# Strassen products also in the down projection of the second MoE, for two couples of token blocks

## The chip, the cores and the metric

The kernel runs on one core of a Trainium2 chip. The metric is device time in microseconds (us) of one execution; lower is better. The engines are TensorE (PE, matrix products), VectorE (DVE), ScalarE (ACT), GpSimd (POOL) and SyncE (SP, which here issues every DMA). Each of them works through its own queue of instructions in order.

## The reference

Attention with a decaying bias (batch 4, 8 heads, 576 positions, head width 64) gives 2304 tokens of width 512. Two feed-forward layers follow; the change lies in the second.

```python
def _moe_ref(x, w_gate, w_val, w_out, rms_g):          # first MoE, d_ff 1536
    xn = x / rms * rms_g
    g = xn @ w_gate
    silu = g * (1.0 / (1.0 + np.exp(-g)))
    return silu * (xn @ w_val) @ w_out
...
def _moe2_ref(x, w_in, w_out):                          # second MoE, d_ff 2048
    h = x @ w_in                                        # 512 -> 2048
    g = h - np.tanh(h)
    return g @ w_out                                    # 2048 -> 512
```

## The kernel before

The tokens are cut into 6 blocks of 384 (`NBLK`, `TB`), held transposed: features on the 128 partitions, 384 tokens in the columns. Every operand of a large product is split into two fp16 halves, and `mm3` (L692) makes a product as three matmuls of 128x128 weights by 384 columns: high by high, high by low, low by high. In code order the attention's last tiles and blocks 0 to 5 of the first MoE come first, then the second MoE. A scheduler in the framework reorders instructions within what data and buffers allow when the program is built, and the order it fixes is the order of the queues; `order` in the section on the change is that order.

**First MoE.** `up1_g` and `up1_v` make one 128-row piece of the hidden layer each (12 matmuls); the DVE ends each by one operation on the temporary `tm` (L712, L722), ACT takes the high half `sh` (L723) and POOL the low half `sl` (L724). `down1` makes an output piece from 36 matmuls and stores it to DRAM (`x2d`, L734).

**Weights of the second MoE.** `w_in` and `w_out` come as 64-bit floats, 16 pieces each of 128x512 numbers (512 KB a load, L557). `decode` turns a piece into fp32 by three DVE operations (L559 to L561); an ACT square (L250) sums it up for a scale; `split` writes the fp16 halves (ACT L575, DVE L576) into the slots of two large tiles, `WI` and `W2`. All of this is a list of small tasks (`w2_tasks`) that are run between the 28 product groups of block 5 of the first MoE, the rest in block 0 of the second.

**Second MoE.** Blocks 0 and 1 are ordinary: `up2` (16 pieces of 12 matmuls; ACT tanh, DVE L1256, ACT high half, DVE L1258 low half into `DH`, `DL`) and `down2` (4 output pieces of 48 matmuls, ACT L1271, store L1272). Blocks 2/3 and 4/5 are taken as couples. On the way up `pair_up` uses Strassen's scheme with seven products in place of eight for the 2x2 blocks of weights and tokens: for each of 8 pieces `s8` seven products of 6 matmuls, put together by DVE (L1302), tanh on ACT (L1288), DVE L1289, high half ACT L1290, low half POOL L1291. The sums of weight blocks that it needs (S1 to S4) are made by DVE from the halves (`form_tasks`, L1182 and on) into the tile `SF`, the sums of token blocks by `x2_forms`. On the way down the couples use the ordinary `down2`, 2 blocks x 4 pieces x 48 = 384 matmuls a couple.

Strassen's scheme in this form makes four output blocks from seven products: one product of the sums S1 and T1 goes into two of the outputs, S2 and S3 likewise.

## Time and profile before

| | us |
|---|---|
| median of 3 runs | 1069.54 |
| lowest, highest | 1068.47, 1090.91 |
| span of the profiled execution | 1066.9 |
| median less span | 2.6 |
| PE busy | 971.0 |
| DVE busy | 680.1 |
| ACT busy | 606.2 |
| POOL busy | 325.6 |

The span runs from the first to the last instruction of the profiled execution. Matmuls overlap in the pipeline of the PE, so the mean length of a row (0.33 us) is twice the step from one matmul to the next. An engine's idle time matters only where a later engine had to wait for it.

### The profile page before, as it was taken

Reading aid. Unit: us, or ns where it says so; the run is one execution under the profiler, and the core shown is the slowest. Engines: PE = TensorE matmul, PEld = TensorE weight load, DVE = VectorE, ACT = ScalarE, POOL = GpSimd, SP = SyncE. Lnnn points to the kernel's source line nnn. Section 1 sums busy time; section 2 is a strip of 40 time slices with the busy share of each in tenths; the row PEclk is TensorE's granted clock in tenths of the full one; section 3 lists DMA queues with packets and bytes.
Section 4 is the critical chain, followed back from the end, with each engine's and each line's share of the span. In section 5 each row is a group of like instructions: output and inputs, shape, how many; then the busy total and the mean of one; then the engine's idle time right before and its main releaser. Section 6 shows DMA issues by size and latency. Waiting matters only on the chain.

```text
span 1066.9 us, 19296 instructions
## 1 busy us (share of the span) xinstructions
PE 971.0 (91%) x7471; PEld 616.9 (58%) x7472; DVE 680.1 (64%) x1472; ACT 606.2 (57%) x1172; POOL 325.6 (31%) x405
## 2 busy tenths in 40 slices
PE   1488967798899999999999899999999999999998
PEld 1377645455566666666667555655666666666664
DVE  8986998975585641674553878579792683438500
ACT  6589657776665763776766446446571462225400
POOL 5121275423462541364356112100200251015200
PEclk9986989999999999999999999999999999999999
DMA  8614524241211112210100960131102000000000
GB/s 269 257 36 108 191 72 144 65 132 38 64 27 53 25 44 74 77 28 21 54 19 11 309 233 1 46 135 68 60 1 82 8 2 16 23 23 1 8 23 30
DMA packets 49439, 76.81 MB, mean 72 GB/s; under 512 B 25891, under 2 KB 35203, under 8 KB 48835
## 3 DMA queue, kind: packets, MB, share of 16 engines
q1 hardware_dynamic: 49346, 75.58, 22.7%
q8 instruction: 58, 0.95, 0.4%
q14 instruction: 35, 0.28, 0.1%
HBM read 59.42 MB, written 9.55 MB: 65 GB/s over the span
## 4 chain that ended last, share of the span: by engine, by line
PE 63%; DVE 15%; DMA 9%; ACT 6%; issue 4%; POOL 2%; SPq 1%; ACTq 0%; DVEq 0%; POOLq 0%
PE m L693 11%; PE m L695 11%; PE m L694 11%; PE mm L693 7%; PE mm L695 7%; PE mm L694 7%; DVE w L560 1%; PE pv L494 1%; PE st L452 1%; PE st L453 1%; DMA wo<-wv 1%; DMA raw<-wo 1%; DMA w<-wo 1%; DVE w L559 1%; DMA qst<-qa 1%
## 5 line engine op out<-in xcount | busy, mean ns | idle before, releaser
L693 PE MATMUL mm<-xth,w 128*128 128x384 f16 x480 | 158.0, 329 | 28.2 <-DVE tm L712 20.9
L694 PE MATMUL mm<-xtl,w 128*128 128x384 f16 x480 | 157.9, 329 | 0.6 <-DMA xtl<-xl 0.6
L695 PE MATMUL mm<-xth,w 128*128 128x384 f16 x480 | 157.5, 329 | 0.1
L694 PEld LDWEIGHTS <-w 128*128 128x128 f16 x960 | 94.4, 98 | 87.1 <-issue 32.7
L693 PEld LDWEIGHTS <-w 128*128 128x128 f16 x960 | 94.9, 99 | 62.7 <-ACT w L575 3.7
L695 PEld LDWEIGHTS <-w 128*128 128x128 f16 x960 | 94.2, 98 | 63.5 <-issue 2.5
L693 PE MATMUL m<-dh,w 128*128 128x384 f16 x384 | 124.0, 326 | 0.7 <-ACT t L1271 0.7
L694 PE MATMUL m<-dl,w 128*128 128x384 f16 x384 | 124.4, 326 | 0.0
L695 PE MATMUL m<-dh,w 128*128 128x384 f16 x384 | 124.0, 326 | 0.0
L474 POOL TENSOR_TENSOR phl<-pf,phl 128x512 f16<-128x512 f32 (+2 forms) x90 | 97.8, 1094 | 40.1 <-ACT phl L467 38.7
L724 POOL TENSOR_TENSOR sl<-tm,sh 128x384 f16<-128x384 f32 x72 | 74.8, 1039 | 112.9 <-ACT sh L723 105.6
L462 POOL TENSOR_SCALAR_AFFINE_SELECT pf<-pf 128x128 f32<-128x128 f32 (+3 forms) x105 | 46.9, 449 | 175.0 <-ACT pf L460 174.7
L1263 POOL TENSOR_SCALAR io<-iso,isd 128x1 f32<-128x1 f32 x24 | 12.0, 501 | 258.8 <-ACT t L1271 258.8
L460 ACT ACTIVATE pf<-st,lnp,ilam 128x512 f32<-128x512 f32 (+2 forms) x105 | 73.0, 703 | 23.0 <-PE st L453 17.9
L1271 ACT ACTIVATE t<-m,io 128x384 f32<-128x384 f32 x24 | 13.8, 578 | 126.1 <-PE m L695 123.0
L693 PE MATMUL mm<-sh,wo 128*128 128x384 f16 x240 | 77.9, 326 | 2.3 <-DVE tm L712 2.3
L695 PE MATMUL mm<-sh,wo 128*128 128x384 f16 x240 | 78.1, 326 | 0.5 <-DVE wo L576 0.5
L694 PE MATMUL mm<-sl,wo 128*128 128x384 f16 x240 | 78.1, 326 | 0.0
L452 PE MATMUL st<-q,kl 128*128 128x128 f16 (+1 forms) x456 | 62.9, 217 | 8.6 <-DVE q L368 2.7
L1302 DVE SCALAR_TENSOR_TENSOR c<-m,sigma,c 128x768 f32<-128x768 f32 x32 | 32.5, 1015 | 57.3 <-PE m L695 55.6
L1291 POOL TENSOR_TENSOR dl<-c,dh 128x768 f16<-128x768 f32 x28 | 48.0, 1731 | 54.9 <-ACT dh L1290 54.9
L712 DVE SCALAR_TENSOR_TENSOR tm<-tm,mm 128x384 f32<-128x384 f32 x60 | 32.8, 547 | 43.9 <-ACT tm L711 41.4
(369 smaller groups left out, 2582.1 us busy)
## 6 DMA issues: line engine op xcount, KB each, us to landing
raw<-wo SPq DMA_DIRECT2D x16, 512.0 KB
w<-win SPq DMA_DIRECT2D x16, 512.0 KB
wo<-wg SPq DMA_DIRECT2D x12, 512.0 KB
wo<-wv SPq DMA_DIRECT2D x12, 512.0 KB
stk<-kt SPq DMA_DIRECT2D x4, 1152.0 KB
x2d<-tm SPq DMA_DIRECT2D x24, 192.0 KB
x2f<-x2d SPq DMA_DIRECT2D x6, 768.0 KB
out<-t SPq DMA_DIRECT2D x24, 192.0 KB
```

Source lines behind the costliest of these rows:

```text
L452: P.matmul(out=ps[:, o:o + w], lhsT=K2[sl][:, ks], rhs=q2_of(T)[:, h, 0:w], start=True, stop=False)
L460: A.activation(out=pf[:, 0:o], in_=ps[:, 0:o], func=ACTF.Exp, scale=bstate[b]["ilam"][:, hh:hh + 1], bias=lnp)
L462: G.affine_select(out=dg, in_=dg, pattern=[[0, len(heads)], [1, w]], compare_op=ALU.is_ge, fill=0.0, base=0, channel_multiplier=-1)
L474: G.tensor_tensor(out=u["pl"][:, 0:n], in0=u["pf"][:, 0:n], in1=u["ph"][:, 0:n], op=ALU.subtract)
L693: P.matmul(out=ps, lhsT=wh, rhs=xh, start=first, stop=False)
L694: P.matmul(out=ps, lhsT=wh, rhs=xl, start=False, stop=False)
L695: P.matmul(out=ps, lhsT=wl, rhs=xh, start=False, stop=last)
L712: V.scalar_tensor_tensor(out=t, in0=t, scalar=1.0, in1=ps, op0=ALU.add, op1=ALU.mult)
L724: moe_pend.append(lambda: G.tensor_tensor(out=SH["l"][:, f, :], in0=t, in1=SH["h"][:, f, :], op=ALU.subtract))
L1271: A.activation(out=t, in_=ps, func=ACTF.Copy, scale=io)
L1291: by.tensor_tensor(out=DL[:, s8, ds, :], in0=c[:, ds], in1=DH[:, s8, ds, :], op=ALU.subtract)
L1302: V.scalar_tensor_tensor(out=out, in0=ps, scalar=sg, in1=c0, op0=ALU.mult, op1=ALU.add)
```

## The change

The couples' down projection is made by Strassen's scheme too (`pair_down`): seven products, each for two output pieces `e` and of 24 matmuls, 336 in place of 384 a couple. That needs the sums of `w_out`'s blocks, and sums of the blocks of the gated hidden layer (`g_forms`). All forms of the weights are now made once, from the fp32 pieces rather than from the halves, written to DRAM (`keep_form`: 28 stores of 256 KB into `wi_d`, 28 into `wo_d`) and read back for the couples through three rotating buffers each (`wr`, 917 KB a load, 16 loads; `wd`, 1 MB, 14 loads). 24 fp32 pieces are parked in DRAM (`pk_d`, 256 KB each) and read again when their sums are made (`sum_tasks`). The sums are cut into tasks, and `newest` makes the scheduler place each behind the newest instruction of DVE and ACT. The order becomes up of block 0, up of block 1, down of block 0, down of block 1, then the couples. Products that are added up stay in one PSUM bank (`acc`), others get banks of their own. WI and W2 take memory in which the normalised tiles `xh`, `xl` of the attention lie.

```diff
+    pk_d = [dram.tile([128, 512], FP32, name=f"pk{i}") for i in range(24)]
+    wi_d = [dram.tile([4, 128, 7, 2, 256], FP16, name=f"wid{i}") for i in range(2)]
+    wo_d = [dram.tile([128, 2, 8, 256], FP16, name=f"wod{i}") for i in range(7)]
...
+    def put(to, t, s):
+        t4 = t.rearrange("p (c w) -> p c w", c=4)
+        A.activation(out=to[:, :, 0, :], in_=t4, func=ACTF.Copy, scale=s)
+        V.scalar_tensor_tensor(out=to[:, :, 1, :], in0=t4, scalar=s, in1=to[:, :, 0, :], op0=ALU.mult, op1=ALU.subtract)
+
+    def keep_form(i, g, k, q, t):
+        if i == 0:
+            SY.dma_start(out=wi_d[g][:, :, q, k].rearrange("c p w -> p c w"), in_=t.rearrange("p c h w -> p c (h w)"))
+        else:
+            SY.dma_start(out=wo_d[q][:, g, 4 * k:4 * k + 4], in_=t.rearrange("p c h w -> p c (h w)"))
...
+        def piece(i, g, k):
+            W, n = (WI, W2)[i], slot_of(g, k)
+            if i == 0:
+                raw = raw_slots(W2, 2 * (n % 4))
...
+            decode(slot_f(W, n), (win, wo2)[i][g, :, k], raw)
...
+            if i == 1 or g % 2:
+                SY.dma_start(out=parked(i, g, k), in_=slot_f(W, n))
...
+        def load(i, g, k):
+            for nm, gg, kk in (("a21", g + 2, k), ("a22", g + 2, k + 2), ("a11", g, k), ("a12", g, k + 2)):
+                d[nm] = in_p.tile([128, 512], FP32, name=nm, tag=nm)
+                SY.dma_start(out=d[nm], in_=parked(i, gg, kk))
...
+        def first(i, g, k):
+            d["t"] = in_p.tile([128, 512], FP32, name="sft", tag="sft")
+            G.tensor_tensor(out=d["t"], in0=d["a21"], in1=d["a22"], op=ALU.add)
+            G.tensor_tensor(out=d["a21"], in0=d["a11"], in1=d["a21"], op=ALU.subtract)
...
+        def third(i, g, k):
+            V.tensor_tensor(out=d["t"], in0=d["t"], in1=d["a11"], op=ALU.subtract)
+            form(i, g, k, S2, d["t"])
+            V.tensor_tensor(out=d["a12"], in0=d["a12"], in1=d["t"], op=ALU.subtract)
+            form(i, g, k, S4, d["a12"])
...
+    def newest():
+        st = ExitStack()
+        for e in (V, A):
+            st.enter_context(tc.issue_after(next(i for i in reversed(nc.cur_bb.bb.instructions) if i.engine == e.engine)))
+        return st
...
+    for f in range(16):
+        up2(0, f)
+        run_tasks(w2t, 1)
...
+    for f in range(16):
+        up2(1, f)
+        if f % 2:
+            with newest():
+                run_tasks(sums, 1)
+    for i, d in enumerate(D_ORDER):
+        with newest():
+            run_tasks(sums, 3)
+        down2(0, d)
+        if i == 0:
+            x2_stat(2)
+        if i == 1:
+            x2_forms(2)
...
+    def g_forms(p, s8):
+        c = CR[:, c_at(p, s8)]
+        V.tensor_tensor(out=c[:, 0:2], in0=c[:, 1:4:2], in1=c[:, 0:2], op=ALU.subtract)
+        V.tensor_tensor(out=c[:, 3], in0=c[:, 3], in1=c[:, 0], op=ALU.subtract)
+        V.tensor_tensor(out=c[:, 2], in0=c[:, 2], in1=c[:, 3], op=ALU.subtract)
+        t = g_form(p, s8)
+        A.activation(out=t[:, :, 0, :], in_=c, func=ACTF.Copy)
+        for e, fs in ((V, slice(0, 2)), (G, slice(2, 4))):
+            e.tensor_tensor(out=t[:, fs, 1, :], in0=c[:, fs], in1=t[:, fs, 0, :], op=ALU.subtract)
+
+    DOWN = [(A11, "h", 0), (A12, "h", 2), (S4, "h", 1), (S2, "t", 3), (S3, "t", 1), (S1, "t", 0), (A22, "t", 2)]
+
+    def load_down(n):
+        if n < 14:
+            wd[n] = wd_p.tile([128, 2, 8, 256], FP16, name="wd", tag="wd")
+            SY.dma_start(out=wd[n], in_=wo_d[DOWN[n % 7][0]])
...
+        acc, fourth = [bank(ps_x) for _ in range(2)], [banks() for _ in range(2)]
+        for i, (q, kind, f) in enumerate(DOWN):
+            w = wd[7 * p + i]
+            for e in range(2):
+                s = st[e]
+                ps = acc[e] if q in (A11, S2, S3, A22) else fourth[e][:, 0] if q == S4 else bank()
+                for s8 in range(8):
+                    v = HL[:, s8, f] if kind == "h" else g_form(p, s8)[:, f]
+                    mm3(ps, w[:, e, s8, 0:128], w[:, e, s8, 128:256], v[:, 0, :], v[:, 1, :], s8, s8 == 0 and q not in (S2, S3, A22), s8 == 7, True)
...
+            if i < 3:
+                with newest() if i == 0 else ExitStack():
+                    for s8 in ((1, 2, 3), (4, 5), (6, 7))[i]:
+                        g_forms(p, s8)
+            load_down(7 * p + i + 3)
```

The order of the queues shows the move at three places. The line numbers are those of each kernel's own code (L557 before is L547 after, L712/L722 before are L702/L712 after).

**SP, at the first loads of w_in.** `w` with a number is the tile W2, in whose slots the raw words land; `xth`, `xtl` are the attention's transposed halves. Before:

```order
L547 DMA_TRANSPOSE xth<-xh 128x4x128
L548 DMA_TRANSPOSE xtl<-xl 128x4x128
L557 DMA w_8286<-win 128x1024 x11
L547 DMA_TRANSPOSE xth<-xh 128x4x128
L557 DMA w_8286<-win 128x1024
L548 DMA_TRANSPOSE xtl<-xl 128x4x128
L557 DMA w_8286<-win 128x1024 x2
L734 DMA x2d<-tm 128x384
L557 DMA w_8286<-win 128x1024
L1091 DMA x2f<-x2d 128x1536
L557 DMA w_8286<-win 128x1024
L734 DMA x2d<-tm 128x384 x2
```

After; `pk` are the parked pieces:

```order
L537 DMA_TRANSPOSE xth<-xh 128x4x128
L538 DMA_TRANSPOSE xtl<-xl 128x4x128
L547 DMA w_8331<-win 128x1024 x7
L724 DMA x2d<-tm 128x384
L547 DMA w_8331<-win 128x1024 x4
L724 DMA x2d<-tm 128x384
L547 DMA w_8331<-win 128x1024
L1046 DMA pk_116<-wi 128x512
L547 DMA w_8331<-win 128x1024
L1046 DMA pk_117<-wi 128x512
L547 DMA w_8331<-win 128x1024
L1046 DMA pk_118<-wi 128x512
```

The eleven loads that stood ahead of the last tile's two transposes stand behind them, and stores of parked pieces stand between the later loads.

**DVE, from block 4 to block 5 of the first MoE.** L559 to L561 before, L549 to L551 after, are the decoding of w_in; L543, L544 the last tile's normalisation, L1052 the first step of w_in's scale. Before:

```order
L559 TENSOR_SCALAR wi<-w_8286 128x512
L561 SCALAR_TENSOR_TENSOR wi<-w_8286,wi 128x512
L543 TENSOR_SCALAR ss<-ss 128x1
L561 SCALAR_TENSOR_TENSOR wi<-w_8286,wi 128x512
L712 SCALAR_TENSOR_TENSOR tm<-tm,mm 128x384
L560 SCALAR_TENSOR_TENSOR wi<-w_8286,wi 128x512
L559 TENSOR_SCALAR wi<-w_8286 128x512
L544 SCALAR_TENSOR_TENSOR ss<-ss 128x1
L559 TENSOR_SCALAR wi<-w_8286 128x512
L722 SCALAR_TENSOR_TENSOR tm<-tm,mm 128x384
L561 SCALAR_TENSOR_TENSOR wi<-w_8286,wi 128x512
```

After:

```order
L549 TENSOR_SCALAR wi<-w_8331 128x512
L550 SCALAR_TENSOR_TENSOR wi<-w_8331,wi 128x512
L551 SCALAR_TENSOR_TENSOR wi<-w_8331,wi 128x512
L702 SCALAR_TENSOR_TENSOR tm<-tm,m_8338 128x384
L712 SCALAR_TENSOR_TENSOR tm<-tm,m_8370 128x384
L549 TENSOR_SCALAR wi<-w_8331 128x512
L550 SCALAR_TENSOR_TENSOR wi<-w_8331,wi 128x512
L551 SCALAR_TENSOR_TENSOR wi<-w_8331,wi 128x512
L702 SCALAR_TENSOR_TENSOR tm<-tm,m_8395 128x384
L712 SCALAR_TENSOR_TENSOR tm<-tm,m_8422 128x384
L1052 TENSOR_REDUCE nm_8464<-px 128x1
```

Before, the first MoE's `tm` operations stand among the decoding of single pieces. After, fifteen pieces are decoded in a row (their last rows stand first here), and the block's first `tm` operations stand behind them.

**ACT, in the down projection of the first couple.** Before, the scaling of output pieces (L1271) and the next couple's token forms (L1140) stand there, behind the last halves of the way up (L1290):

```order
L1290 ACTIVATE dh<-c_10787 128x2x384
L1290 ACTIVATE dh<-c_10787 128x768
L1271 ACTIVATE t_10897<-m_10848,io 128x384
L1271 ACTIVATE t_10950<-m_10848,io 128x384
L1271 ACTIVATE t_11004<-m_10955,io 128x384
L1140 ACTIVATE xf<-x2f,x2s 128x768 x7
L1271 ACTIVATE t_11057<-m_10955,io 128x384
```

After, the kept products (L1437) and the high halves of the hidden sums (L1408) stand among one another:

```order
L1437 ACTIVATE s_11146<-px,io_10034 128x384
L1437 ACTIVATE s_11172<-px,io_10034 128x384
L1408 ACTIVATE cr<-cr 128x4x384 x3
L1437 ACTIVATE m_11288<-m_11120,io_10034 128x384
L1408 ACTIVATE cr<-cr 128x4x384
L1437 ACTIVATE m_11314<-m_11121,io_10034 128x384
L1408 ACTIVATE cr<-cr 128x4x384 x3
L1437 ACTIVATE u_11354<-px,io_10034 128x384
L1437 ACTIVATE u_11381<-px,io_10034 128x384
```

The kept product `m` of S4 now stands between high halves of the hidden sums, and those stand behind the first two kept products.

## Rows read from the trace of the kernel before

Of a row of windows, the columns are: stretch in us, its length, then busy us (and instructions) of PE, its weight loads, DVE, ACT and POOL, then the granted clock of the PE, the DMA engines' busy share and GB/s. Of a group's row, the columns are: line, engine, operation, output<-inputs, shapes and count | busy us, mean ns of one | idle us of the engine before them <-what ended it.

**Rows 1.** The page, part 1: busy us (share) and instructions.

```profile
PE 971.0 (91%) x7471; PEld 616.9 (58%) x7472; DVE 680.1 (64%) x1472; ACT 606.2 (57%) x1172; POOL 325.6 (31%) x405
```

**Rows 2.** The page, part 4: the chain of waits by engine.

```profile
PE 63%; DVE 15%; DMA 9%; ACT 6%; issue 4%; POOL 2%; SPq 1%; ACTq 0%; DVEq 0%; POOLq 0%
```

**Rows 3.** Windows by stage of the second MoE.

```profile
699.00:734.50 35.50, 32.48 (x200) 19.30 (x198) 33.90 (x68) 23.18 (x48) 0.00 (x0) 1.00 0.36 125
831.20:882.90 51.70, 51.70 (x321) 31.12 (x319) 42.74 (x45) 31.11 (x40) 22.04 (x14) 1.00 0.01 5
882.90:945.00 62.10, 62.10 (x385) 37.53 (x384) 18.54 (x25) 14.61 (x20) 4.59 (x9) 1.00 0.06 23
```

**Rows 4.** Waits of PE, 588 to 700 us: total, times, longest.

```profile
PE mm L693 <- DVE tm L712: 2.9, 2, 1.4
PE m L693 <- DVE tm L712: 2.8, 2, 2.4
```

**Rows 5.** Window of the w_in loads.

```profile
588.00:612.00 24.00, 21.12 (x130) 12.51 (x129) 21.00 (x47) 11.14 (x29) 4.28 (x3) 1.00 0.97 319
```

**Rows 6.** Timeline of PE: start, length, [idle before].

```profile
594.46 0.32 PE L693 MATMUL mm<-xth,w 128*128 128x384 f16 x1 [1.44 <-DVE tm L712]
...
598.20 0.33 PE L695 MATMUL mm<-xth,w 128*128 128x384 f16 x1
599.96 0.32 PE L693 MATMUL mm<-sh,wo 128*128 128x384 f16 x1 [1.44 <-DVE tm L712]
...
699.02 0.33 PE L693 MATMUL m<-x2f,wi 128*128 128x384 f16 x1
...
1063.15 0.33 PE L695 MATMUL m<-dh,w 128*128 128x384 f16 x1
```

**Rows 7.** Timeline of SP, 586 to 606 us: its issues.

```profile
587.69 12.87 SPq L557 DMA_DIRECT2D w<-win  x11
...
605.21 1.19 SPq L548 DMA_TRANSPOSE xtl<-xl  x1
```

**Rows 8.** Groups of DVE, 590 to 700 us.

```profile
L576 DVE SCALAR_TENSOR_TENSOR wi<-wi,si 128x512 f16<-128x512 f32 x16 | 12.0, 748 | 3.5 <-ACT wi L575 3.2
```

**Rows 9.** Timeline of DVE at three places.

```profile
649.07 0.75 DVE L576 SCALAR_TENSOR_TENSOR wi<-wi,si 128x512 f16<-128x512 f32 x1 [0.33 <-ACT wi L575]
649.74 0.55 DVE L722 SCALAR_TENSOR_TENSOR tm<-tm,m 128x384 f32<-128x384 f32 x1
...
670.87 0.54 DVE L722 SCALAR_TENSOR_TENSOR tm<-tm,m 128x384 f32<-128x384 f32 x1
671.33 0.55 DVE L712 SCALAR_TENSOR_TENSOR tm<-tm,m 128x384 f32<-128x384 f32 x1
...
707.92 0.42 DVE L559 TENSOR_SCALAR w<-raw 128x512 int32<-128x512 int32 x1
708.25 0.68 DVE L560 SCALAR_TENSOR_TENSOR w<-raw,w 128x512 int32<-128x512 int32 x1
708.85 0.61 DVE L1256 SCALAR_TENSOR_TENSOR t<-m,u,t 128x384 f32<-128x384 f32 x1
709.38 0.68 DVE L1197 TENSOR_TENSOR xf<-wi,xf 128x512 f32<-128x512 f16 x1
```

**Rows 10.** Groups of DVE, 831 to 945 us.

```profile
L1289 DVE SCALAR_TENSOR_TENSOR c<-ta,nsd,c 128x768 f32<-128x768 f32 x16 | 19.3, 1214 | 0.8 <-ACT ta L1288 0.7
L1302 DVE SCALAR_TENSOR_TENSOR c<-m,sigma,c 128x768 f32<-128x768 f32 x17 | 17.3, 1015 | 52.0 <-PE m L695 50.3 <-ACT xf L1133 1.1
...
L1146 DVE TENSOR_TENSOR x2f<-x2f 128x768 f32<-128x768 f32 x1 | 1.0, 951 | 0.0
```

**Rows 11.** Groups of POOL, 831 to 945 us.

```profile
L1291 POOL TENSOR_TENSOR dl<-c,dh 128x768 f16<-128x768 f32 x14 | 24.5, 1768 | 28.7 <-ACT dh L1290 28.7
```

**Rows 12.** Groups of ACT, 831 to 945 us.

```profile
L1133 ACT ACTIVATE xf<-x2f 128x1536 f16<-128x1536 f32 x2 | 3.0, 1475 | 0.0
```

**Rows 13.** The chain of waits in order of time.

```profile
1.25 5.11 DMA stk<-kt
...
699.83 1.82 DMA x2d<-tm
```

More of the change, by code (lines that the diff above doesn't have):

```diff
@@ L105, in tile_forget_attention_moe_moe2 @@
     wide = [None]
[L106 to L112 removed]
     def mm_tile():
[L116 removed]
+        if wide[0] is not None:
             return wide[0].tile([128, 512], FP32, name="m2", tag="m2", bufs=4)[:, 0:TB]
[L118 to L122 removed]
         return ps_mm.tile([128, 512], FP32, name="mm", tag="mm")[:, 0:TB]
@@ new lines, in flat, with form, sums @@
+        def flat(n):
+            return W2[:, n, :].bitcast(FP32)
+        def form(g, k, q, t, n):
+            put(slot4(W2, n), t, sc[0][:, g:g + 1])
+            keep_form(0, g, k, q, slot4(W2, n))
+        def sums(g, k, part):
+            a11, a12, a21, a22 = (slot_f(WI, slot_of(gg, kk)) for gg in (g, g + 2) for kk in (k, k + 2))
+            t, u = flat(8 + 2 * k), flat(9 + 2 * k)
+            if part == 0:
+                G.tensor_tensor(out=t, in0=a21, in1=a22, op=ALU.add)
+                G.tensor_tensor(out=u, in0=a11, in1=a21, op=ALU.subtract)
+            elif part == 1:
+                form(g, k, S1, t, 12)
+                form(g, k, S3, u, 13)
+            else:
+                V.tensor_tensor(out=t, in0=t, in1=a11, op=ALU.subtract)
+                form(g, k, S2, t, 14)
+                V.tensor_tensor(out=t, in0=a12, in1=t, op=ALU.subtract)
+                form(g, k, S4, t, 15)
@@ L1272, in down2, with load_up @@
         SY.dma_start(out=out[j, d], in_=t)
+    wr, wd = {}, {}
+    def load_up(n):
+        if n < 16:
+            wr[n] = wr_p.tile([128, 7, 2, 256], FP16, name="wr", tag="wr")
+            SY.dma_start(out=wr[n], in_=wi_d[n % 8 // 4][n % 4])
+    D_ORDER = (0, 2, 1, 3)
+    x2_prep(1)
+    for f in range(16):
+        up2(0, f)
+        run_tasks(w2t, 1)
+    for i in range(2, 4):
+        x2_load(i)
+    run_tasks(w2t, 1000)
+    st_ws.close()
+    st_sf = ctx.enter_context(ExitStack())
+    sums = sum_tasks(pool(st_sf, "in", bufs=1, side="right"), pool(st_sf, "fo", bufs=3, side="right"))
@@ new lines, in tile_forget_attention_moe_moe2 @@
+    for f in range(16):
+        up2(1, f)
[6 more added lines that the diff above has]
+        down2(0, d)
+        if i == 0:
+            x2_stat(2)
+        if i == 1:
+            x2_forms(2)
+    for n in range(3):
+        load_up(n)
+    for i, d in enumerate(D_ORDER):
+        with newest():
+            run_tasks(sums, 2)
+        down2(1, d)
+    for st in (st_sf, st_a, st_d, st_pm):
+        st.close()
@@ L1353, in tile_forget_attention_moe_moe2 @@
+    run_tasks(sums, 1000)
+    for n in range(3):
+        load_down(n)
+    for j in (2, 4):
+        if j == 2:
+            x2_load(4)
+            x2_load(5)
+        pair_up(j)
+        pair_down(j)
+    for st in (st_pm, st_m2, st_w2):
         st.close()
```

428 lines of the change are left out of this document (207 added, 221 removed).

## The prediction, made before the changed kernel had run

> **What bounds the kernel now.** I read the page first: PE is busy for 91% of the span [rows 1], and most of the chain of waits is PE, with DVE a distant second [rows 2]. So matmuls that go are time that goes, where PE is the engine that ends last; where DVE is, they are not. The windows tell the two apart. In the couples' stages PE is busy without a gap (51.70 of 51.70 us, 62.10 of 62.10) while DVE has room, much of it on the way down (18.54 of 62.10) [rows 3]. In block 0 of the second MoE it is the other way: DVE 33.90 of 35.50 us and PE 32.48 [rows 3]. Before that, where w_in is decoded, DVE is busy 21.00 of 24 us and the DMA engines 97% of the time at 319 GB/s [rows 5], and PE loses 2.9 + 2.8 us waiting for the DVE's `tm` [rows 4].
>
> The step from one matmul to the next is (598.20 - 594.46) / 23 = 0.1625 us [rows 6]. I check it on the whole second MoE: from its first matmul at 699.02 [rows 6] 768 matmuls of blocks 0 and 1 take 124.8 us, 1440 of the couples 234.0, which makes 1057.8; the last one starts at 1063.15 [rows 6], so all waits from 699 on are some 5.5 us. Behind the last matmul's start come 0.16 us for itself and 3.6 us to the end of the span at 1066.9. The median of the runs lies 2.6 us above the span, and I carry that over.
>
> **The change, part by part.**
>
> *Matmuls removed.* Two couples x (384 - 336) = 96, at 0.1625 us: 15.6 us. The couples then cost 1344 x 0.1625 = 218.4 us. This is on the path: PE has no gap there now [rows 3].
>
> *The front (loads of w_in and block 5 of the first MoE).* Before, eleven loads went out from 587.69 on, ahead of the last tile's transposes, whose second was issued at 605.21 [rows 7]. After, they stand behind both transposes. The norm and the transposes (1.19 us to issue one [rows 7]) have nothing in front of them any more, so I let the loads start at 595, between the bounds 590 and 605. What is to land before the fifteenth piece is decoded is 15 x 0.524 + 6 parked pieces x 0.262 + 3 tiles of x2d x 0.197 = 10.0 MB; at 319 GB/s [rows 5] 31.4 us, so 626.4, and with its decoding 628. In return DVE is free for block 4: the waits of 1.44 us at 594.46 and 599.96 [rows 6] go, block 4 ends at 620.5 instead of 623.4, and PE, four tiles ahead of DVE at most, runs until about 628 before it has to wait for the `tm` operations behind the fifteen decodings. So there is nothing or little to wait there, if the rate holds; at 268 GB/s it is 5.7 us.
>
> From 628 on DVE is the bound. In its row stand 24 `tm` operations at a step of 0.46 (670.87 to 671.33), 9 decodings at 0.33 + 0.60 + 0.60 (the middle row's step for each of the last two), 19 low halves at 0.67 (649.07 to 649.74) [rows 9], 4 sums at 0.60 and 22 small ones that I put at 0.13 us: 11.0 + 13.8 + 12.7 + 2.4 + 2.9 = 42.8 us. Low halves wait for ACT's high halves; before, sixteen of them waited 3.5 us in all [rows 8], so 4.2 at the least for 19; ACT has the new forms beside them, so I take 7. The last `tm` is then through at 677.8, its low half `sl` 2 us later at 679.8. `down1` has 36 matmuls (5.85 us) to do before it needs that, and lasts 144 x 0.1625 = 23.4 us: the second MoE starts at 679.8 - 5.85 + 23.4 = 697.4, against 699.02 before. The bounds: 691 if PE never waits there, 706 if the loads come at 268 GB/s and the waits for ACT are 12 us.
>
> *Blocks 0 and 1, up.* Both are now in one piece, with 8 decodings of w_out, 14 low halves and the forms beside them. Taking the DVE's row in order at the steps above (0.53 for L1256 [rows 9], 0.9 for an operation of 768 columns [rows 10]), its 28th tile is through at 61.6 us and its 32nd at 70.4, PE's at 54.6 and 62.4. PE may be four tiles (7.8 us) ahead, and 24 matmuls of `pair_up` are drawn ahead of the last ones. By the sum DVE is just in time; for its waits for ACT I take 2 us of loss (0 to 8). The 5.5 us of waits that stood here and at the end before are replaced by that.
>
> *Sums and stores.* The POOL additions, the stores of 56 forms and the 24 loads of parked pieces lie in stages where DMA was busy 36% of the time and POOL not at all [rows 3], and behind them. I put them at nothing, with the down products of blocks 0 and 1 (62.4 us of PE, in which DVE has only the token forms and half of the sums) as cover; if that cover were gone, their DVE part, 24 low halves at 0.67 us [rows 9], would cost 16 us.
>
> *The way up of the couples.* DVE had 42.74 of 51.70 us [rows 3], 45.1 in a full 54.6; about two g_forms' worth of work is added (0.95 + 2 x 0.5 + 0.95 us for one whole and subtractions of others [rows 10]), 8.5 us: 53.6 of 54.6. It holds, barely.
>
> *The way down of the couples.* The first three products need only halves that are there; the forms are needed from 23.4 us on. A form costs DVE about 1.95 + 0.95 us, ACT 1.5 (1536 columns [rows 12]) and POOL 1.77 [rows 11]; if engines overlap, some 3 us each for six left, 18 us: in time. ACT also frees the PSUM banks of S4 (L1437), which stand behind high halves, so DVE's lateness would reach PE. S1's weights are only asked for when S4 has left its buffer, and 1 MB lands 5 to 6 us later (1152 KB took 5.11 [rows 13]), about 1 us behind the point at which PE's row first uses them. I take 1 us each and 0.5 for small sums: 2.5 (0 to 5).
>
> At this place a rule speaks against the change. DVE's L1289, both of whose inputs lie in SBUF, took 1214 ns in the mean beside POOL's L1291, while L1302 of the same size with one input in PSUM kept 1015 [rows 10, 11]. The Trainium skill, "SBUF — State Buffer", section "Who interferes with whom", says that a DVE instruction with two SBUF inputs contends with a GpSimd instruction that reads SBUF, the two taking the shared port pair in turns; the rows agree in kind, at 0.2 us an operation. If every form's low half on DVE stood wholly behind POOL's, it would be rival 2 below; by the measured 0.2 us it is 6 operations x 0.2, about 1 us a couple, inside the bounds.
>
> *The sum:* 697.4 + 124.8 + 2 + 218.4 + 2.5 + 3.6 = 1048.7 of span, plus 2.6: **1051 us**, 18 less than before.
>
> **The rivals.**
>
> *Rival 1: DVE does not bound the front.* If ACT's and DVE's halves interleave better than I charge and the loads land early, block 5 runs at PE's pace and the second MoE starts at 691 to 694: 1044 to 1048. For it: the old conversions waited only 3.5 us in all [rows 8]. Against: the sum of the row has no slack in it.
>
> *Rival 2: late forms in the way down.* If the steps of a form follow one another, DVE, ACT, then DVE's and POOL's low halves in turn (1.95 + 1.5 + 0.95 + 1.77 = 6.2 us), six forms take 37 us where 23.4 + 7.8 = 31.2 are there before S2's last matmuls; with the halves of the last piece ahead of them that is 5 to 9 us a couple, 10 to 18 in all: 1061 to 1069. This is the case in which the change doesn't do what it says: the matmuls are saved and come back as waits. For it: ACT's row puts S4's kept product among the high halves. Against: DVE is free for two thirds of that stage [rows 3].
>
> *Rival 3: slower than before, by the traffic at the front.* The loads now share the queue with parked pieces, and behind them with stores of forms in 512-byte rows. If all that moves at below about 190 GB/s, the 10 MB take 53 us and more; the fifteenth piece is decoded at 650, PE waits 22 us from 628 on, and the rest of the row follows: 1051 + 22 = 1073. It decides from that rate, about 0.6 of what the trace shows [rows 5]. Against: the old stretch held its 319 GB/s with x2d stores and transposes between. A store's price is seen at 1.82 us for x2d [rows 13], which others don't wait for.
>
> **How the numbers follow.** A measurement of this kernel can tell about 2% from no change: below 1048.1 is faster, above 1090.9 slower. The forecast (1046 to 1058) has 0.50, rival 1 0.22, rival 2 0.18, rival 3 0.10. Faster by over 2%: all of rival 1 and a fifth of the forecast, 0.32. Slower by over 2%: the part of rival 3 in which the rate is below 140 GB/s (10 MB in 71 us, 40 us of waits, 1091), 0.04. Within: 0.64. The range leaves out rival 3 and the outer edges of 1 and 2: 1042 (start at 691, 2 us of waits in all: 691 + 343.2 + 2 + 3.6 + 2.6) to 1067 (rival 2 at 16 of its 18 us).
>
> **What the profile after would show.** The couples in 218 to 223 us from first to last matmul; the first `up2` matmul at 695 to 699; w_in's fifteenth decoding ending near 628 and PE's waits for `tm` between there and 680; PE's waits in the two up blocks under 8 us. Waits of PE for `cr` (L1408, L1410) above 3 us a couple would mean rival 2; a gap of PE over 10 us near 630, rival 3. I would be wrong beyond these if the stores of forms and their reading back made PE wait for `wr` or `wd`, which I put at 1 us a couple.

## The result, and the profile after

The changed kernel takes 1080.14 us in the median of four runs (1077.56 to 1080.49), the kernel before 1069.72: a ratio of 1.0109, 95% interval 1.0087 to 1.0131. One execution of the kernel before, of 1090.91 us, was in the chip's slower state, and the ratio leaves it out. The changed kernel is slower by about 1%, where 18 us less had been forecast; the range ended at 1067. The profiled execution has a span of 1075.8 us.

The 96 matmuls are gone. Had nothing else moved, that alone would be 15.6 us less; so some 25 us came back as waits. The page of the changed kernel, part 1 and the chain of waits [rows 1, 2]:

```profile
PE 964.3 (90%) x7371; PEld 607.5 (56%) x7372; DVE 742.8 (69%) x1538; ACT 637.9 (59%) x1212; POOL 367.2 (34%) x421
...
PE 43%; DVE 21%; DMA 14%; issue 9%; ACT 8%; POOL 5%; SPq 1%; ACTq 0%; DVEq 0%; POOLq 0%
```

PE is busy for 6.7 us less than before, not for 15.6. Of the 8.9 us between, 3.0 lie ahead of 590 us (509.95 us busy against 506.96), before the first load of w_in goes out; the rest lies behind it, where the changed kernel has more waits and slow steps, and a matmul that no other follows at once counts its whole 0.33 us. So this number is no measure of the steps saved. PE's share of the chain fell from 63% to 43%, DVE's rose from 15 to 21%, that of DMA from 9 to 14%: the end is set more often by handing over from engine to engine.

PE's waits from 560 us to the end (total us, times, longest):

```profile
PE m L683 <- DVE tm L702: 8.8, 4, 6.3
PE px L684 <- POOL cr L1410: 6.2, 5, 1.7
PE m L683 <- DVE t L1264: 5.2, 6, 2.0
PE m L683 <- DVE tm L712: 1.6, 2, 1.2
...
PE px L683 <- ACT cr L1408: 1.4, 2, 0.7
```

Before, the whole list for the same place in the program was 2.9 + 2.8 + 2.5 + 0.6 + 0.7 us. Timeline of PE, five rows that bound the stages and show the longest waits [rows 6]:

```profile
636.28 0.48 PE L683 MATMUL m<-xth,w 128*128 128x384 f16 x1 [6.31 <-DVE tm L702]
636.56 0.52 PE L684 MATMUL m<-xtl,w 128*128 128x384 f16 x1
...
707.11 0.33 PE L683 MATMUL m<-x2f,wi 128*128 128x384 f16 x1
...
779.52 0.32 PE L683 MATMUL m<-xf,wi 128*128 128x384 f16 x1 [1.99 <-DVE t L1264]
...
1072.12 0.33 PE L685 MATMUL px<-cr,wd 128*128 128x384 f16 x1
```

The second MoE starts at 707.11, not at 697.4 as forecast (before 699.02). The last matmul starts at 1072.12 in place of a forecast 1044.9. By stages, with the steps of 0.1625 us taken off, the difference to the sum of the forecast is:

| stage | forecast | measured | off by |
|---|---|---|---|
| start of the second MoE | 697.4 | 707.1 | +9.7 |
| loss in blocks 0 and 1 (waits, slow steps) | 2.0 | 9.9 | +7.9 |
| loss in the couples | 2.5 | 12.1 | +9.6 |

Here a loss is the stage's length less its matmuls times 0.1625 us (768 and 1344; 23 of the couples' run ahead of block 1's last one and are counted there). The three add up to 27.2, and 1048.7 + 27.2 is the measured span.

**The front.** SP's issues of the loads of w_in, and what its loads waited for [rows 7]:

```profile
595.06 1.25 SPq L538 DMA_TRANSPOSE xtl<-xl  x1
596.37 11.51 SPq L547 DMA_DIRECT2D w<-win  x7
608.02 0.34 SPq L724 DMA_DIRECT2D x2d<-tm  x1
609.09 9.35 SPq L547 DMA_DIRECT2D w<-win  x4
618.58 0.34 SPq L724 DMA_DIRECT2D x2d<-tm  x1
621.05 0.33 SPq L547 DMA_DIRECT2D w<-win  x1
622.86 0.33 SPq L1046 DMA_DIRECT2D pk<-wi  x1
623.67 0.33 SPq L547 DMA_DIRECT2D w<-win  x1
...
630.04 0.44 SPq L547 DMA_DIRECT2D w<-win  x1
```

```profile
SPq L547 <- ACT w L240: 17.8, 11, 3.6
```

The transposes are out at 596.3 as expected. But seven loads take 11.5 us and four more 9.35, and SP waits 17.8 us in all for ACT's squares (L240), which are the last to use a raw slot. The window from the first load to the last, and three windows behind it (columns as in [rows 3, 5]):

```profile
596.40:630.50 34.10, 32.90 (x202) 19.57 (x201) 24.21 (x40) 10.87 (x29) 7.40 (x6) 1.00 0.76 253
...
760.00:792.00 32.00, 27.50 (x155) 15.53 (x154) 30.54 (x46) 23.95 (x40) 2.86 (x2) 0.95 0.53 170
846.00:902.00 56.00, 55.57 (x344) 33.58 (x344) 52.09 (x69) 29.32 (x41) 22.33 (x15) 1.00 0.53 192
902.00:960.00 58.00, 53.58 (x326) 31.74 (x325) 32.01 (x44) 24.29 (x28) 16.88 (x7) 1.00 0.40 140
```

The loads move at 253 GB/s with the DMA engines busy for 0.76 of the time, where before it was 319 at 0.97 [rows 5]: for the time that the engines are busy both are some 330 GB/s, so they were not slower, they had less to do. The 10.0 MB of the forecast take 39.6 us at this rate in place of 31.4. So the fifteenth decoding ended not at 628 but here, on DVE, with block 5's first `tm` operation right behind it:

```profile
635.08 0.69 DVE L551 SCALAR_TENSOR_TENSOR wi<-w,wi 128x512 int32<-128x512 int32 x1
635.68 0.55 DVE L702 SCALAR_TENSOR_TENSOR tm<-tm,m 128x384 f32<-128x384 f32 x1
636.34 0.56 DVE L712 SCALAR_TENSOR_TENSOR tm<-tm,m 128x384 f32<-128x384 f32 x1
```

and PE waited 6.31 us for the first of these two. PE also ran slower behind the wait: the next matmuls step by 0.28 to 0.32 us (the first two are among the PE rows above), and the granted clock just behind the wait,

```profile
636.00:643.00 7.00, 6.72 (x29) 3.71 (x29) 5.64 (x14) 3.97 (x10) 2.11 (x2) 0.65 0.29 111
```

is 0.65, a mixture of the two levels, 1.2 and 2.4 GHz; ten steps at 0.32 and three near 0.28 in place of 0.1625 are 1.9 us. This did not delay the second MoE: it starts 71.3 us after the end of the fifteenth decoding (635.77 to 707.11), and the same 71.3 us after it in e7_early below (630.50 to 701.79), where PE waits only 0.65 us and the granted clock stays at 1.00. In both, PE waits for DVE's `tm` twice more in this stretch (1.19 and 1.51 us near 670 and 674 here, 1.17 and 1.51 there). The forecast had 69.4 us for the stretch; so of the 9.7 us, 7.8 are the late decoding.

**Blocks 0 and 1.** In the window from 760 to 792 DVE is busy 30.54 of 32 us and PE only 27.50; PE waits for `t` of L1264, up to 1.99 us.

**The way down.** The windows from 846 and from 902: on the way up DVE is at 52.09 of 56 us and PE at 55.57 without a loss worth naming, as forecast; on the way down DVE has room (32.01 of 58), POOL 16.88 and ACT 24.29, and still PE loses. One form's chain there, timelines of ACT, DVE and POOL:

```profile
916.29 1.48 ACT L1408 ACTIVATE cr<-cr 128x1536 f16<-128x1536 f32 x1 [2.52 <-POOL cr L1410]
920.29 1.48 ACT L1408 ACTIVATE cr<-cr 128x1536 f16<-128x1536 f32 x1 [2.52 <-POOL cr L1410]
...
917.80 0.96 DVE L1410 TENSOR_TENSOR cr<-cr 128x768 f16<-128x768 f32 x1 [2.52 <-ACT cr L1408]
...
917.85 2.41 POOL L1410 TENSOR_TENSOR cr<-cr 128x768 f16<-128x768 f32 x1 [1.59 <-ACT cr L1408]
```

ACT's next high half waits 2.52 us for POOL. The halves of a form are written over the piece that the form before still reads, so ACT (1.48 us) and POOL (2.41) take turns, one form each 4.00 us. Of the 14 POOL operations of 128x768 behind the mean of 1.77 us in [rows 11], twelve took 1.63 to 1.75 us and two took 2.41; beside DVE's low half, which starts 0.05 us ahead of it, each of these here takes 2.41.

### The profile page after: what moved, and what is told of

Its sections match the earlier page's. It is cut to its first block, busy times and chain, and to the rows that moved or that the text cites. A ratio compares the mean times of both kernels' runs of the same rounds, so it can differ in the third digit from the quotient of the medians.

```text
span 1075.8 us, 19578 instructions
## 1 busy us (share of the span) xinstructions
PE 964.3 (90%) x7371; PEld 607.5 (56%) x7372; DVE 742.8 (69%) x1538; ACT 637.9 (59%) x1212; POOL 367.2 (34%) x421
## 4 chain that ended last, share of the span: by engine, by line
PE 43%; DVE 21%; DMA 14%; issue 9%; ACT 8%; POOL 5%; SPq 1%; ACTq 0%; DVEq 0%; POOLq 0%
PE mm L683 7%; PE mm L685 7%; PE mm L684 7%; DVE cr L1352 4%; PE m L683 3%; PE m L684 3%; PE m L685 3%; POOL cr L1410 2%; DMA w<-win 2%; DMA w<-wo 2%; DMA x2f<-x2d 2%; DVE cr L1359 2%; PE pv L484 1%; PE st L442 1%; PE st L443 1%
## 5 line engine op out<-in xcount | busy, mean ns | idle before, releaser
L683 PE MATMUL mm<-xth,w 128*128 128x384 f16 x480 | 159.5, 332 | 24.2 <-DVE tm L702 16.1
L685 PE MATMUL mm<-xth,w 128*128 128x384 f16 x480 | 159.2, 333 | 0.0
L684 PEld LDWEIGHTS <-w 128*128 128x128 f16 x704 | 69.8, 99 | 74.9 <-issue 37.9
L452 POOL TENSOR_SCALAR_AFFINE_SELECT pf<-pf 128x128 f32<-128x128 f32 (+3 forms) x105 | 43.8, 419 | 174.5 <-ACT pf L450 173.9
L685 PEld LDWEIGHTS <-w 128*128 128x128 f16 x704 | 69.7, 99 | 48.3 <-issue 4.6
L683 PEld LDWEIGHTS <-w 128*128 128x128 f16 x704 | 70.2, 100 | 47.3 <-issue 4.1
L1363 POOL TENSOR_TENSOR hl<-cr,hl 128x768 f16<-128x768 f32 (+1 forms) x28 | 39.1, 1414 | 91.6 <-ACT hl L1362 68.2
L702 DVE SCALAR_TENSOR_TENSOR tm<-tm,mm 128x384 f32<-128x384 f32 x60 | 32.9, 548 | 47.0 <-ACT tm L701 39.0
L443 PE MATMUL st<-qc,kc 128*128 128x128 f16 (+1 forms) x456 | 58.7, 214 | 0.6 <-DMA qc<-rt 0.6
L1410 POOL TENSOR_TENSOR cr<-cr 128x768 f16<-128x768 f32 x16 | 37.7, 2359 | 54.9 <-ACT cr L1408 54.9
L1358 ACT ACTIVATE ta<-cr,isd 128x768 f32<-128x768 f32 (+1 forms) x34 | 30.4, 896 | 43.6 <-DVE cr L1352 41.4
L457 ACT ACTIVATE phl<-pf 128x512 f16<-128x512 f32 (+2 forms) x90 | 49.4, 557 | 10.6 <-PE pv L488 5.3
L713 ACT ACTIVATE sh<-tm 128x384 f16<-128x384 f32 x72 | 37.1, 517 | 29.3 <-DVE tm L712 29.2
L442 PEld LDWEIGHTS <-kl 128*128 128x128 f16 x480 | 44.8, 103 | 13.6 <-DVE kl L288 7.8
```

The costliest lines, as they stand in the source:

```text
L442: P.matmul(out=ps[:, o:o + w], lhsT=K2[sl][:, ks], rhs=q2_of(T)[:, h, 0:w], start=True, stop=False)
L443: P.matmul(out=ps[:, o:o + w], lhsT=KC[sl][:, ks], rhs=qc_of(T)[:, h, 0:w], start=False, stop=True)
L452: G.affine_select(out=dg, in_=dg, pattern=[[0, len(heads)], [1, w]], compare_op=ALU.is_ge, fill=0.0, base=0, channel_multiplier=-1)
L457: A.activation(out=ph[:, 0:o], in_=pf[:, 0:o], func=ACTF.Copy)
L683: P.matmul(out=ps, lhsT=wh, rhs=xh, start=first, stop=False, skip_group_check=free)
L684: P.matmul(out=ps, lhsT=wh, rhs=xl, start=False, stop=False, skip_group_check=free)
```

## The experiments

The theories A, H and D say that three separate places cost the time: the loads of w_in (late start and four raw slots), DVE's load in the up products, and the chain of the forms. The rivals say that traffic sets the rate, or that DVE does throughout. Ratios are to the kernel before, run beside each (the changed kernel: 1.0109). Two things limit what one run can tell. The profiled executions differ by chance before the first load already: the same matmul of block 4 starts at 593.88 in the changed kernel and between 592.41 and 597.87 in the others. And the scheduler fixes the order of the queues anew for every edit, so no run changes one cause with all else held.

**e1_ring8.** Eight raw slots for the first eight pieces.

```diff
-                raw = raw_slots(W2, 2 * (n % 4))
+                raw = raw_slots(W2, 2 * (n % 8 if n < 8 else n % 4))
```

> The first eight pieces of w_in get eight raw slots in place of four; nothing else changes. Theory A (the ring of four raw slots holds up the loads: a load waits for the square of the piece four before it): the loads go out from 596.4 at about 1.6 us each, the fifteenth decoding ends near 630 instead of 635.7, and the time falls by 4 to 6 us from 1080 to about 1075. Rival B (the traffic itself, with parked pieces and stores, limits the rate): under 1 us of change.

Measured 1074.76 us, ratio 1.0053 [1.0037, 1.0069]. Its SP issue, PE's wait at the place, what SP's loads waited for, and the window from the first load to the last:

```profile
598.27 11.57 SPq L547 DMA_DIRECT2D w<-win  x11
...
632.33 0.32 PE L683 MATMUL m<-xth,w 128*128 128x384 f16 x1 [1.28 <-DVE tm L702]
```

```profile
SPq L547 <- ACT w L240: 7.6, 7, 2.7
```

```profile
598.30:625.00 26.70, 26.70 (x166) 16.07 (x165) 22.27 (x40) 10.88 (x29) 14.20 (x5) 1.00 0.88 320
```

Eleven loads go out in the time in which seven did, the same bytes move at 320 GB/s, the fifteenth decoding ends at 631.68, PE waits 1.28 us instead of 6.31, and the second MoE starts at 702.5, although this execution stood 1.9 us later at block 4's matmul. The slots held up the loads; the traffic did not.

**e7_early.** WI and W2 lie where they lay before the change, as one tile in which CR and a part of HL are views later on.

```diff
-    x2_p = pool(st_w2, "x2", bufs=2, side="right")
-    sc_p = pool(st_w2, "sc", bufs=2, side="right")
-    st_a = ctx.enter_context(ExitStack())
-    w2 = pool(st_a, "w2", side="right")
-    WI = w2.tile([128, 17, 1024], FP16, name="wi")
-    W2 = w2.tile([128, 17, 1024], FP16, name="w2")
+    w2 = pool(st_w2, "w2", side="right")
+    WW = w2.tile([128, 34, 1024], FP16, name="ww")
+    WI, W2 = WW[:, 0:17], WW[:, 17:34]
+    x2_p = pool(st_w2, "x2", bufs=2, side="right")
+    sc_p = pool(st_w2, "sc", bufs=2, side="right")
...
+    CR = WW[:, 0:27].rearrange("p a w -> p (a w)").bitcast(FP32).rearrange("p (s a t) -> p s a t", s=9, a=4)
```

> WI and W2 lie where they lay before the change (ahead of the x2 tiles), as one tile, in which CR and part of HL are views later; the ring keeps four slots. Theory A (the loads start late because their memory is still held by the last normalised tile): the first load goes out near 588 instead of 596.4, the fifteenth decoding ends 7 to 9 us earlier, the time falls by 6 to 9 us to about 1072. Rival B (rate-limited): the loads start early but end at the same time, under 2 us.

Measured 1071.86 us, ratio 1.0034 [1.0010, 1.0059]. The first load goes out at 588.6, PE's wait at 633 is 0.65 us, and the second MoE starts at 701.8: a gain of the size that the ring brought, by the other half of the same cause.

**e8_early_ring.** Both edits together.

> Both: memory as before the change and eight raw slots. Theory A: the fifteenth decoding near 622, the second MoE starts about 12 us earlier (near 700), time about 1067 to 1069. Rival B: above 1076. Rival C (DVE is the bound of the whole front, wherever the loads stand): gains stop at about 5 us, 1075.

Measured 1075.45 us, ratio 1.0056 [1.0035, 1.0078]. The two remedies do not add, against theory A's 1067 to 1069. Rival B's "above 1076" cannot be told apart by the time, whose interval is 1073.0 to 1077.6 us, but e1_ring8 has refuted it; rival C's number fits. SP's issues show where it stuck:

```profile
588.74 12.90 SPq L547 DMA_DIRECT2D ww<-win  x11
...
604.18 1.31 SPq L547 DMA_DIRECT2D ww<-win  x1
...
618.48 0.33 SPq L547 DMA_DIRECT2D ww<-win  x1
```

The thirteenth load goes out at 618.48, 14 us behind the twelfth and only 5 us ahead of the changed kernel's (623.67), and PE waits 2.75 us at 635.5.

**e10_park.** As e8_early_ring, but the parked pieces of w_in are stored from ACT's queue.

```diff
-                SY.dma_start(out=parked(i, g, k), in_=slot_f(W, n))
+                (A if i == 0 else SY).dma_start(out=parked(i, g, k), in_=slot_f(W, n))
```

> As early_ring, but the eight parked pieces of w_in are stored from ACT's queue, behind the square of the same piece, in place of SP's. Theory K (in early_ring the last loads of w_in stand in SP's queue behind parked stores that wait for the decoding, so the fifteenth decoding did not come earlier): the last load goes out near 612 instead of 623, the fifteenth decoding ends near 626, PE's wait of 2.75 us at 635 goes, and the time is 1068 to 1071 against early_ring's 1075. Rival B (rate): as early_ring, 1073 to 1076.

Measured 1074.42 us, ratio 1.0045 [1.0030, 1.0060]. Theory K falls: with no parked store in SP's queue any more the thirteenth load still goes out at

```profile
603.79 0.42 SPq L547 DMA_DIRECT2D ww<-win  x1
...
618.10 0.33 SPq L547 DMA_DIRECT2D ww<-win  x1
```

618.10. The pieces from the ninth on share four slots in both kernels, and their squares come when DVE has decoded them, among block 4's `tm` operations. That these slots and DVE's order are what is left is read from the trace; no run changed them.

**e4_split.** On the way down, DVE makes three quarters of a form's low halves.

```diff
-        for e, fs in ((V, slice(0, 2)), (G, slice(2, 4))):
+        for e, fs in ((V, slice(0, 3)), (G, slice(3, 4))):
```

> In the way down of the couples DVE makes three quarters of a form's low halves and POOL one (before two and two). Theory D (a form's high half waits until POOL has read the place it overwrites, so ACT and POOL make a chain of 4.0 us a form): the step becomes about 3.0 us, the waits of PE for POOL there fall from 6.2 us in all to under 1.5, the time by 5 to 8 us to about 1074. Rival E (the forms are late because their chain starts late, behind DVE's subtractions): the step may shrink but PE's waits stay above 4 us, under 2 us of time.

Measured 1075.92 us, ratio 1.0077 [1.0055, 1.0098]: 3 to 4 us less, not 5 to 8, and the interval overlaps that of the changed kernel. The step is 3.68 us, not 3.0, and PE's waits for POOL are 5.4 us, not under 1.5; the loss in the couples falls from 12.1 to 9.4 us. So theory D has the direction and not the size. The groups of POOL and DVE in this kernel's first way down:

```profile
L1410 POOL TENSOR_TENSOR cr<-cr 128x384 f16<-128x384 f32 x7 | 14.6, 2085 | 24.7 <-ACT cr L1408 24.7
...
L1410 DVE TENSOR_TENSOR cr<-cr 128x1152 f16<-128x1152 f32 x7 | 9.5, 1359 | 13.5 <-ACT cr L1408 13.4
```

POOL's half as large operation still takes 2085 ns, in place of 2411. It starts 0.05 us behind DVE's operation of 1.36 us and ends 0.77 us after it; in the changed kernel it ends 1.50 us after DVE's (920.26 against 918.76). So the part behind DVE's end goes with POOL's columns (0.77 us for 384, 1.50 for 768): these times are as if POOL did nearly all of its work when DVE is through.

**e5_dveonly.** All low halves of the forms on DVE.

```diff
-        for e, fs in ((V, slice(0, 2)), (G, slice(2, 4))):
+        for e, fs in ((V, slice(0, 4)),):
```

> All low halves of a form on DVE, none on POOL; the place that a form overwrites is the same. Theory D2 (ACT's next high half waits for the last reader of the place that it overwrites, and DVE and POOL there wait for each other, 2.41 us together): the chain's step becomes 1.48 + about 1.8 + 0.15 = 3.4 us instead of 4.0, DVE's operation of 1536 columns takes 1.8 us with nothing beside it, and the time falls by 6 to 8 us to about 1073. Rival F (POOL is needed: DVE becomes the bound of that stage): no change or slower.

Measured 1068.09 us, ratio 1.0002 [0.9985, 1.0018]: 11 to 12 us less than the changed kernel, more than expected; 8.4 of it lie in the couples. Its profiled execution also starts the second MoE 2 us sooner, but 1.5 of these it had at block 4's matmul already, ahead of anything that the edit touches. ACT's and DVE's rows:

```profile
914.07 1.48 ACT L1408 ACTIVATE cr<-cr 128x1536 f16<-128x1536 f32 x1 [1.89 <-DVE cr L1410]
...
917.44 1.48 ACT L1408 ACTIVATE cr<-cr 128x1536 f16<-128x1536 f32 x1 [1.41 <-DVE cr L1410]
...
915.59 1.76 DVE L1410 TENSOR_TENSOR cr<-cr 128x1536 f16<-128x1536 f32 x1 [1.08 <-ACT cr L1408]
...
932.42 1.76 DVE L1410 TENSOR_TENSOR cr<-cr 128x1536 f16<-128x1536 f32 x1 [1.61 <-ACT cr L1408]
```

The step is 3.37 us, and all 1536 columns on DVE alone take 1.76 us, less than the 2.41 us of half of them on POOL beside it. The loss in the couples falls from 12.1 to 3.7 us. Rival F falls.

**e6_ten.** Ten places in CR, so that a form overwrites nothing that the form before reads; halves two and two as in the changed kernel. To make room, one kept product shares the buffers of another temporary.

```diff
-    CR = c_p.tile([128, 9, 4, TB], FP32, name="cr")
+    CR = c_p.tile([128, 10, 4, TB], FP32, name="cr")
...
-        return (9 - p + s8) % 9
+        return (8 * p + s8) % 10
```

> Ten places in the ring CR in place of nine, so that a form is written two places behind and not over the piece that the form before still reads; the halves stay two and two on DVE and POOL. Theory D2: ACT no longer waits for POOL, the step falls to POOL's own 2.4 us, PE's waits for forms to under 2 us in all, and the time by 8 to 11 us to about 1070. Rival G (the pair of DVE and POOL is the chain, whatever the place): the step stays near 4 us and the time within 2 us.

Measured 1074.61 us, ratio 1.0043 [1.0026, 1.0060]: 5 to 7 us less, not 10, and PE's waits for forms stayed at 6.5 us; the loss in the couples falls from 12.1 to 8.7 us. POOL's row, and one of DVE's:

```profile
914.23 16.31 POOL L1410 TENSOR_TENSOR cr<-cr 128x768 f16<-128x768 f32 x7 [15.04 <-ACT cr L1408]
...
918.19 1.58 DVE L1410 TENSOR_TENSOR cr<-cr 128x768 f16<-128x768 f32 x1 [0.73 <-ACT cr L1408]
```

Seven operations in 16.31 us, back to back, 2.33 each. ACT now waits 0.8 us for the form two behind in place of 2.52, as theory D2 has it, and the pair of DVE and POOL becomes the chain, as rival G said, though not at its 4 us. The two take turns: DVE's operation, 0.96 us in the changed kernel, now takes 1.58 and ends 0.82 us after POOL's, POOL's ends 1.50 us after DVE's, and 0.82 + 1.50 is the step. So each was half right: the place that is overwritten made 4.00 out of 2.33, and the 2.33 comes from DVE and POOL beside each other.

The step alone does not set PE's loss, though. The last form is ready at 930.54 here and only at 934.18 in e5_dveonly, and yet PE loses 8.7 us here and 3.7 there. In this kernel's PE queue the first 48 matmuls that read forms stand in a row; in e5_dveonly another product comes in after 30 of them, in the changed kernel after 32. What that order is worth is open, since no run holds it fixed.

**e9_held.** The token forms of couple 2/3 are held to the place at which the code makes them.

```diff
         if i == 1:
-            x2_forms(2)
+            with newest():
+                x2_forms(2)
```

> The token forms of couple 2/3 are held behind the newest instruction at the place where the code makes them (the down products of block 0), in place of among the up products of block 1. Theory H (DVE is overloaded in the up products of blocks 0 and 1 by work that has until the couples): PE's waits for L1264 fall from 5.2 to about 2, the time by 2 to 4 us to about 1077. Rival: the couples' first products then wait for the forms, no gain.

Measured 1073.02 us, ratio 1.0051 [1.0027, 1.0075]: 6 to 7 us less, twice the expectation. The same window as above, and PE's waits for L1264 in blocks 0 and 1:

```profile
760.00:792.00 32.00, 31.72 (x196) 18.93 (x194) 25.65 (x43) 21.85 (x38) 8.30 (x6) 1.00 0.62 202
```

```profile
PE m L683 <- DVE t L1264: 1.0, 3, 0.5
```

DVE is down to 25.65 of 32 us, PE up to 31.72, the loss in both blocks falls from 9.9 to 2.8 us, and nothing later waits for the forms.

**e11_best, e12_ring_best.** The token forms held and all low halves on DVE, with the early memory order (e11) or with eight raw slots (e12) for the front.

> Three of the remedies together: WI and W2 where they lay before the change, the token forms held, all low halves of the forms on DVE. If the causes are separate places (front 5 us, up products 6 us, way down 8 us), the sums add: second MoE from about 702, blocks 0 and 1 some 6 us shorter, the couples at 218 to 220 us, 1059 to 1062 in all, faster than the kernel before by about 0.8%. If they share one cause (each only moves a wait to the next place), it stays at 1066 or above.

> The same with eight raw slots in place of the old memory order: 1059 to 1063 if the remedies add, about equal to the other combination, since either alone brought 5 to 8 us at the front.

Measured 1055.77, ratio 0.9889 [0.9869, 0.9909], and 1055.91, ratio 0.9890 [0.9862, 0.9917]. The places are separate: the gains add, to 3 us more than expected.

**e14_nofront.** The same two remedies, the front as changed.

> The changed kernel with the token forms held and all low halves of forms on DVE, the front as it is. If the parts add: 1080 less 12 (DVE alone) less 7 (held) = 1061 to 1063, 5 to 7 us above e11_best. If the front's lateness is made up later, 1057.

Measured 1062.95, ratio 0.9955 [0.9937, 0.9972], as the sum of the parts had it; so the front is worth 7 us of the whole (1062.95 - 1055.8), and it is not made up later.

**e13_n5, e15_ring_n5.** e11 and, in the second, e12, with eight of w_out's tasks moved from block 5 into block 0's up products.

```diff
-    n5 = n_in + 17
+    n5 = n_in + 9
...
-        run_tasks(w2t, 1)
+        run_tasks(w2t, 2 if f < 9 else 1)
```

> The first combination, and 8 of the 17 tasks of w_out that ran in block 5 of the first MoE moved into the up products of block 0. If DVE's load between 640 and 690 is what still holds the front, PE's 4 us of waits for tm there go and the second MoE starts 2 to 4 us earlier (698 to 700), at the price of some waits in block 0's up products: net 0 to -3 us. If it is only moved, it is slower by up to 3 us.

> As e13_n5 with eight raw slots in place of the old memory order: 1053 to 1055, the same within 2 us, if eight slots and an early start are two remedies for one wait.

Measured 1053.39, ratio 0.9869 [0.9849, 0.9889], and 1052.01, ratio 0.9853 [0.9838, 0.9869]: the lowest median of all, 1.5% below the kernel before. The intervals overlap those of e11_best and e12_ring_best, so the moved tasks' 2 to 4 us are barely clear of noise; the second MoE does start earlier, at 699.0 and 698.4 against 702.8 and 701.9. What is left of PE's waits in it from 585 us to the end (its three longest totals):

```profile
PE m L683 <- DVE tm L702: 3.2, 3, 1.7
PE m L683 <- DVE t L1264: 1.8, 2, 1.3
PE px L684 <- DVE cr L1411: 1.5, 2, 1.3
```

**b2_x2first, b1_ring4, b3_both.** One part of the change at a time in the kernel before: the x2 tiles placed ahead of WI and W2 (late start of the loads, eight slots); four slots in place of eight (early start); both.

> The kernel before with one part of the change alone: the x2 tiles are placed ahead of WI and W2, so that the loads of w_in stand behind the last tile's transposes; eight raw slots as before. Theory A (late loads cost time by themselves): the loads start near 596, DVE's decoding comes later, slower by 3 to 8 us. Rival L (the late start is harmless with eight raw slots, since DVE is free for block 4 in return): within 2 us.

> The kernel before with four raw slots for w_in in place of eight, loads early as before. Theory M (four slots are harmful only if the loads also start late: with an early start the decoding keeps up): within 2 us of the kernel before. Rival N (four slots cost by themselves): slower by 3 to 6 us.

> The kernel before with four raw slots and the x2 tiles placed first, so that the loads start late as well. Theory M: slower by 4 to 8 us, like the changed kernel's front. Rival N: as b1_ring4.

Measured 1068.37, ratio 1.0008 [0.9996, 1.0019]; 1066.58, ratio 0.9987 [0.9972, 1.0002]; 1071.06, ratio 1.0027 [1.0012, 1.0042]. Neither alone costs anything that can be told; together they cost about 3 us, with a wait of PE that neither has:

```profile
633.75 0.48 PE L693 MATMUL m<-xth,w 128*128 128x384 f16 x1 [3.06 <-DVE tm L712]
```

That is theory M by its sign. The size is below its 4 to 8 us: in the kernel before the scheduler puts other loads between, so that the two fronts aren't the same otherwise. That the late start alone would be slow (theory A in b2_x2first) is refuted; rival N too. In b1_ring4 the fifteenth decoding ends as late as 634.09, and no wait of PE behind it is above 1 us. There `tm` operations stand between the last decodings; in the changed kernel fifteen decodings stand in a row ahead of block 5's first. That this order is what turns a late load into a wait of PE fits both, but no run changed the order alone.

## Why the prediction was wrong

**The matmuls (15.6 us): right.** In e15_ring_n5 blocks 0 and 1 lose 2.8 us and the couples 2.6, within 1 us of the 2.0 and 2.5 of the forecast's sum. That its 1052.0 us also meets the forecast 1051 is in part luck, since the forecast moved no tasks out of block 5; without that it is 1055.9 (e12_ring_best). The saving was there; what was missed are three ways in which the kernel handed it back.

**The front: the step that failed is "at 319 GB/s, so 626.4".** I took the rate of the window before as the rate of a queue, and did not see in the diff that raw slots for the loads went from eight to four. With four, a load waits for the square of the piece four before it; the rate became 253 GB/s with the engines busy 76% of the time, and the fifteenth decoding ended at 635.8 in place of 628. I had the other half of the cause, the late start, at its right place (595 against 596.4), and it alone costs nothing: in b2_x2first, late with eight slots, the decoding ends at 627.71, where I had put it. My bound for the rate, 268 GB/s with 5.7 us of waits, came near the measured 253 and 6.31, but I gave no cause for it and the sum did not carry it. Rival 3 named the place (PE waits near 630 for the fifteenth decoding) with another cause, the traffic; e1_ring8 refutes that, as the same traffic went through at 320 GB/s. What is left of the front with eight slots, 702.5 for 697.4, is not taken apart by any run: 1.3 us of it this execution had at block 4's matmul already (595.78 for 594.46 in the kernel before), and moving tasks out of block 5 (e15_ring_n5) brings 698.4.

**Blocks 0 and 1: the step "by the sum DVE is just in time" was mis-sized, 9.9 us of loss for 2.** DVE's row ended 8.0 us behind PE's against a lead of 7.8, and I allowed for waits on ACT with 2 us out of a range of 0 to 8. The work that made it tight was not due there: the scheduler had drawn the token forms of the couple into the up products. My row has operations of 768 columns there, which can only be these forms, while my paragraph on sums counts the token forms under the down products; in the trace all eleven of their DVE operations, 10.8 us, end ahead of 785 us. I did not name them as a thing that could be moved, and e9_held, which moves them, brings the loss to 2.8 us.

**The way up: right.** DVE had 52.09 of 56 us, and PE lost nothing worth naming.

**The way down: the step "if engines overlap, some 3 us each" failed.** They don't overlap: ACT must wait for POOL because a form overwrites what the one before reads, and POOL must wait for DVE. The measured step is 4.0 us (e6_ten and e5_dveonly take the two waits apart), between my 3 and rival 2's 6.2; rival 2 was the right mechanism at a smaller price (4.8 us a couple above the forecast, for 5 to 9). Its chance of 0.18 was too low, since the overwriting stands in the changed code (the `8 - p` in the index of g_form beside the `9 - p` of c_at). How much of the step reaches PE hangs on the order of its queue too (e6_ten), and that part stays open.

**The rule that I weighed and discounted.** I took the measured 0.2 us of L1289 beside POOL as the price, 1 us a couple, and looked at DVE alone. The rows of e4_split, e6_ten and the changed kernel show POOL's operation ending 0.77 us (384 columns) and 1.50 us (768) after DVE's, so nearly the whole of it comes behind DVE's. The Trainium skill, "SBUF — State Buffer", section "Who interferes with whom", calls the shared port pair "an exclusive lock", for a DVE instruction with two SBUF inputs against a GpSimd instruction that reads SBUF; these rows agree. Before's trace had shown it too, and on which engine the price falls. Of the 16 operations in the mean of 1214 ns, four found a POOL operation running and took 1206 to 2423 ns. Seven met none, and five began ahead of POOL's; these twelve all took 1002 to 1020. But of the five POOL operations that began behind DVE's, the two that came 0.1 us behind took 2.41 us themselves, like the forms later on. One such pair:

```profile
853.80 1.00 DVE L1289 SCALAR_TENSOR_TENSOR c<-ta,nsd,c 128x768 f32<-128x768 f32 x1
...
853.91 2.41 POOL L1291 TENSOR_TENSOR dl<-c,dh 128x768 f16<-128x768 f32 x1 [1.77 <-ACT dh L1290]
```

So the step that failed here is 0.2 us an operation: the engine that comes second pays, in the forms that is POOL, and it pays some 0.7 us (2.41 against 1.63 to 1.75).

**POOL additions, stores, reading back: right.** No wait of PE names them, `wr` or `wd`.
